# Block 1's second half of attention in 32-query tiles, transposed on VectorE

## The chip, the cores and the metric

The kernel runs on one core of a Trainium2 chip, in one launch. The metric is the device time of that core in microseconds (us). A program that sets out all instructions runs on five engines at once: TensorE (PE, with its weight loads as PEld), VectorE (DVE), ScalarE (ACT), GpSimd (POOL) and SyncE (SP), which here only issues DMAs. Each engine takes its own instructions strictly in order and waits where one of them needs a result of another engine.

## What is computed

Sparse attention, then two MLPs. Of eight heads the first four see a local window, the others a strided set:

```
scores = (1/sqrt(64)) * q @ k.T                     # q, k, v: (4, 8, 576, 64) float32
mask_local   = (rel >= 0) & (rel < 32)              # heads 0 to 3, rel = query - key
mask_strided = (rel >= 0) & (rel % 32 == 0)         # heads 4 to 7
attn = softmax(where(mask, scores, -1e9)) @ v
x = attn as (2304, 512)
x = (s * relu(x @ w_in)**2 + b) @ w_out             # 2048 wide
out = ((x @ w_a) * (x @ w_b)) @ w_out2              # 1536 wide
```

All products of the MLPs are made from pairs of reduced-precision halves: a high part (written by ScalarE) and the remainder (written by VectorE), in three matmul passes.

## The kernel before

**Blocks and calls.** The first MLP runs over five blocks of columns. Block 0 holds the first 128 positions of all four batches (512 columns), blocks 1 to 4 the other 448 positions of one batch each, give or take 64 (block 1 has 384). A block is 16 calls, one for each slice of 128 hidden rows: `h_mm` (12 matmuls into the single bank of `ps_h`, then `relu`, square and the split into `gt`, lines 773 to 789), `o_mm` of two calls earlier (12 matmuls into `acc`), and then `attend`, which runs whatever steps of the attention the plan has for that call.

**Weights.** In block 0 each call also turns two weight pieces from their 64-bit input form into halves: `raw` is scaled on ScalarE (line 130), shifted and merged by VectorE (lines 133, 136, 140), copied as the high half by ScalarE (line 111), and its remainder is taken by VectorE (line 112, `w<-raw,w`). The pieces of call f are used one and two calls later.

**Units.** The attention of a later block is made in six units while the block before it is computed: four local ones (two head pairs, two spans of positions each; `near` in `plan`) and two strided ones (two head pairs, all 448 positions; `far`). A unit is a generator of six or seven steps: loads, transposes of q and k, scores, softmax, softmax, transposes of the probabilities, output. The output goes through `split` into the next block's `x` tile: the high part by ScalarE, the remainder by VectorE.

**Two forms of a unit.** Block 1's units are `local` and `strided`, in 64-query tiles. Their q and k are transposed on TensorE (`pst`, line 97) and copied out of PSUM by ScalarE (lines 294, 337, 351). `local` lets a matmul write the mask into the scores' bank first, takes the maximum on VectorE (line 231) and makes four exponentials with running sums on ScalarE (line 237); `strided` adds the mask on VectorE (line 243) over 2 x 288 columns and goes on with 576-column steps (lines 244 to 254). The units of blocks 2 to 4 are `local_pairs` and `strided_pairs`, in 32-query tiles: q and k are loaded in 32 x 32 blocks and transposed by VectorE (`STREAM_TRANSPOSE`, lines 445, 501, 502), the mask is added on VectorE (line 419), and maximum, subtraction, sum, reciprocal and scaling (lines 426 to 433) stand on VectorE over 256 columns (local) or 288 (strided), with one exponential on ScalarE (line 428). The transposes of the probabilities and the output take fewer, larger or more, smaller matmuls.

**What sets the order.** `plan(n)` gives each unit a first call and a tuple of offsets; step k runs in call first + offset k:

```
near: 4 * i - 1, local(...) if n == 1 else local_pairs(...), at_n     # i = 0 to 3
far:  8 * i + 1, (strided if n == 1 else strided_pairs)(...), at_f    # i = 0, 1
```

TensorE's instructions keep this written order (`in_order`). The other engines' order is set by the scheduler of the framework, from its own estimate of when each instruction becomes ready; SP's too. Below, L1 to L4 stand for the local units `near[0]` to `near[3]` of block 1, S1 and S2 for `far[0]` and `far[1]`.

**Shared room.** PSUM has eight banks: four for `acc`, one for `h`, three for everything of the attention (`ps_a`, tag "a"), which each `pst`, `pss`, `ppt` and `po` takes in turn; a bank is free again when its last reader is done. The `r` tile of `h_mm` is single as well. The local units' `qk` has one buffer, the strided units' `sqk` one.

Of the kernel before, what the change touches and what calls it, by code (L numbers as in the profile page):

```python
# [25 lines left out]
def sparse_attention_two_mlps(  # L26
# [24 lines left out]
    TF = P  # L51
# [41 lines left out]
    def mm(*args, **kwargs):  # L93
        last_pe[:] = [nc.tensor.matmul(*args, **kwargs).ins]  # L94

    def mm_t(*args):
        last_pe[:] = [nc.tensor.transpose(*args).ins]  # L97
# [12 lines left out]
    def split(hi, lo, src):  # L110
        nc.scalar.activation(out=hi, in_=src, func=AF.Copy)  # L111
        return nc.vector.tensor_tensor(out=lo, in0=src, in1=hi.bitcast(F32), op=ALU.subtract)  # L112
# [45 lines left out]
    def x_tile(n):  # L158
        if n not in x_t:
            x_t[n] = xp[n % 2].tile([P, 2, KD, TR if n % 2 else TM], F32R, tag="x", name="x")  # L160
            if n and n % 2 == 0:
                nc.gpsimd.tensor_copy(out=x_t[n][:, :, :, 0:OVER], in_=x_t[n - 1][:, :, :, TR - OVER:])
        return x_t[n]

    def first_column(n):
        return OVER if n % 2 == 0 else 0

    QT = 64
# [89 lines left out]
    def window(src, bb, head, t0, nt):  # L258
        at = src[bb, head, t0:S, :]
        return bass.AP(at.tensor, at.offset, [[D, WK], [QT * D, nt], [1, D]])  # L260
# [10 lines left out]
    def local(bb, n, pair, t0, nt):  # L271

        nq, nk = nt * QT, nt * QT + STR
        mq, mk = (P, nk // 3) if nk % 3 == 0 else (nq // 2, nk // 2)
        cq, ck = nq // mq, nk // mk
        nu = -(-nt // 2)
        tl = lambda shape, name: lp.tile(shape, F32, tag=name, name=name)
        qk = tl([P, 5, 2, D], "qk")
        z = t0 + nq
        qn, kn = qk[:, 0:2], qk[:, 2:]  # L280
        for h in range(2):
            for dst, src, a, m in ((qn, q, t0, mq), (kn, k, t0 - STR, mk)):
                nc.sync.dma_start(
                    out=dst[:m, 0:(z - a) // m, h],
                    in_=src[bb, 2 * pair + h, a:z, :].rearrange("(c p) d -> p c d", p=m),
                )
        yield
        qkT = lp.tile([P, 9 * QT], F32, tag="lT", name="qkT")
        qT, kT = qkT[:, 0:nq], qkT[:, nq:nq + nk]
        for src, m, c, dst in ((qn, mq, cq, qT), (kn, mk, ck, kT)):  # L290
            ps = ps_a.tile([P, c, m], F32, tag="a", name="pst")
            for i in range(c):
                mm_t(ps[:, i], src[:m, i].rearrange("p h d -> p (h d)"), ident[:m, :m])
            nc.scalar.activation(out=dst.rearrange("p (c m) -> p c m", m=m), in_=ps, func=AF.Copy)
        yield
        vn = tl([WK, 4, 2, D], "vn")
        for h in range(2):
            nc.sync.dma_start(out=vn[:, 0:nt, h], in_=window(v, bb, 2 * pair + h, t0 - STR, nt))
        pss = [ps_a.tile([P, nu, WK], F32, tag="a", name="pss") for _ in range(2)]

        def put(alone):
            for j in range(2 * nu if alone else nt):
                i = min(j, nt - 1) * QT
                for h in range(2):
                    hr = slice(h * D, (h + 1) * D)
                    mm(
                        pss[h][j % 2 * QT:(j % 2 + 1) * QT, j // 2],
                        lhsT=qT[hr, i:i + QT], rhs=kT[hr, i:i + WK],
                        start=alone, stop=(alone or j >= nt - 2),
                    )  # L310

        pt = tl([P, 2, nu, WK], "lpt")
        yield from softmax(pt, pss, lmask, put, n == 1, pair == 0 and t0 == TF)
        yield
        ppt = ps_a.tile([WK, 2 * nu, P], F32, tag="a", name="ppt")
        for i in range(2 * nu):
            mm_t(ppt[:, i, :], pt[:, i // nu, i % nu], ident)
        pT = lp.tile([WK, 2, nu * P], F32, tag="lT", name="pT")
        nc.scalar.activation(out=pT.rearrange("p h t -> p (h t)"), in_=ppt.rearrange("p i t -> p (i t)"), func=AF.Copy)
        yield  # L320
        po = ps_a.tile([P, nq], F32, tag="a", name="po")
        for j in range(nt):
            for h in range(2):
                mm(
                    po[h * D:(h + 1) * D, j * QT:(j + 1) * QT],
                    lhsT=vn[:, j, h, :], rhs=pT[:, h, j * QT:(j + 1) * QT],
                    start=True, stop=True,
                )
        xt, c0 = x_tile(n), t0 - TF + first_column(n)
        split(xt[:, 0, pair, c0:c0 + nq], xt[:, 1, pair, c0:c0 + nq], po)  # L330
        yield
# [654 lines left out]
    steps = {}  # L986

    def plan(n):
        at_n = (-2, 0, 1, 1, 2, 3, 4) if n == 1 else (-3, 0, 1, 2, 3, 4)
        at_f = (-3, 0, 1, 2, 4, 5) if n == 1 else (-3, 0, 1, 2, 3, 5)  # L990
        near = [
            (
                4 * i - 1,
                local(0, n, i % 2, TF + i // 2 * 4 * QT, 4 - i // 2) if n == 1
                else local_pairs(n - 1, n, i % 2, TF + i // 2 * 8 * QS, 8 - i // 2 * 2),
                at_n,
            )
            for i in range(4)
        ]
        far = [(8 * i + 1, (strided if n == 1 else strided_pairs)(n - 1, n, i), at_f) for i in range(2)]  # L1000
        if n == 1:
            near[0] = (0, near[0][1], (-5, -3, 0, 1, 1, 2, 3))
            far[0] = (1, far[0][1], (-5, 1, 2, 3, 5, 7))
        if n == 2:
            near[0] = (-1, near[0][1], (-2, 0, 1, 2, 3, 4))
        for first_, gen, at in near + far:
            for t in at:
                steps.setdefault((n - 1) * NF1 + first_ + t, []).append(gen)
# [80 lines left out]
    for n in range(1, NB):  # L1089
        plan(n)  # L1090
# [91 lines left out]
    for pair in range(NP2):  # L1182
        acc = [ps_acc.tile([P, DM], F32, tag="acc", name="acc2") for _ in range(TB2 // P)]
        later_x, late = [], []
        for g in range(NG2):
            i = pair * NG2 + g
# [129 lines left out]
```

## Time and profile before

| | us |
|---|---|
| median of 3 runs (lowest, highest) | 900.36 (900.26, 900.46) |
| profiled execution: span from first to last instruction | 898.1 |
| median less span: lies around the span | 2.3 |
| TensorE busy in the span | 888.6 |
| VectorE busy | 620.5 |
| ScalarE busy | 401.4 |
| first `h` of block 0, first `h` of block 1 | 31.56, 134.13 |

No time of the profiled execution other than its span is listed; the table sets the span beside the median of the runs. Starts in a timeline are measured, the ends of matmuls are modelled, so the length of a piece of TensorE's work is read here from start to start. On VectorE, instructions that follow each other closely overlap by some 0.08 to 0.1 us in the rows: the next one starts that much before the modelled end of the one ahead.

### The profile page before, as it was taken

To read this page: it belongs to the slowest core of one execution; us is meant where nothing else is said; L and a number is where in the kernel's file an instruction comes from. 1 tells how busy PE (TensorE), PEld (TensorE's weight loads), DVE (VectorE), ACT (ScalarE), POOL (GpSimd) and SP (SyncE) were. 2 spreads that over 40 slices of the span, in tenths; PEclk is the share of its full clock that TensorE was granted. 3 is DMA by queue.
4 is the path that set the end of the run, shared out by engine and by line. 5 is a ranking of instruction groups with operands and counts; after the bars stand their busy time and mean duration, and the time that the engine had idled before them with its cause. 6 is when DMAs were issued, how large, how long until landed. Compare 5 with 4: busy or idle time off the path is not lost.

```text
span 898.1 us, 16348 instructions
## 1 busy us (share of the span) xinstructions
PE 888.6 (99%) x6166; PEld 793.8 (88%) x6166; DVE 620.5 (69%) x1263; ACT 401.4 (45%) x866; POOL 42.0 (5%) x120
## 2 busy tenths in 40 slices
PE   8999999999999999999999999999999999999997
PEld 6778889999888899998889999988999988999986
DVE  6898995676766777727665777765776765776741
ACT  6777774434333343353333445354334444333322
POOL 6000000000000010001100000000000000000000
PEclk9999999999999999999999999999999999999999
DMA  9965534656765666446666343423432221433010
GB/s 229 292 204 162 166 77 134 159 149 162 207 170 159 176 190 172 130 137 220 196 214 207 129 141 112 138 80 113 151 99 94 84 94 59 124 95 106 30 36 35
DMA packets 156606, 126.41 MB, mean 141 GB/s; under 512 B 102256, under 2 KB 131440, under 8 KB 156528
## 3 DMA queue, kind: packets, MB, share of 16 engines
q1 hardware_dynamic: 149840, 109.12, 43.3%
q0 software_dynamic: 4608, 15.73, 4.4%
q8 instruction: 48, 0.79, 0.4%
q10 hardware_dynamic: 2080, 0.52, 0.3%
q14 instruction: 30, 0.25, 0.1%
HBM read 100.17 MB, written 25.17 MB: 140 GB/s over the span
## 4 chain that ended last, share of the span: by engine, by line
PE 97%; ACT 2%; DVE 1%; issue 0%; POOL 0%; ACTq 0%; POOLq 0%
PE acc L94 38%; PE pp L94 29%; PE h L94 22%; PE po L94 2%; PE pss L94 1%; PE ppt L97 1%; PE fpo L94 1%; PE fps L97 0%; PE lull L94 0%; ACT raw L130 0%; ACT fpt L596 0%; PE fss L94 0%; PE pst L97 0%; PE fpp L97 0%; PE fpx L97 0%; ACT r L778 0%
## 5 line engine op out<-in xcount | busy, mean ns | idle before, releaser
L94 PE MATMUL pp<-x2w,wf 128*128 128x384 f32 x1512 | 265.8, 335 | 0.0
L94 PEld LDWEIGHTS pp<-x2w,wf 128*128 128x128 f32 x1512 | 263.0, 188 | 1.8 <-ACT u L596 0.4
L94 PE MATMUL h<-x,w 128*128 128x512 f32 (+1 forms) x960 | 217.0, 374 | 0.0
L94 PE MATMUL acc<-gt,w 128*128 128x512 f32 (+2 forms) x960 | 210.7, 368 | 1.0 <-ACT w L111 1.0
L94 PEld LDWEIGHTS acc<-gt,w 128*128 128x128 f32 x960 | 175.5, 188 | 24.1 <-ACT w L111 1.5
L94 PEld LDWEIGHTS h<-x,w 128*128 128x128 f32 x960 | 171.8, 188 | 24.2 <-DVE w L112 0.5
L94 PE MATMUL acc<-o2w,abt 128*128 128x512 f32 x648 | 150.5, 390 | 0.0
L94 PEld LDWEIGHTS acc<-o2w,abt 128*128 128x128 f32 x648 | 121.4, 188 | 24.6
L778 ACT ACTIVATE r<-h 128x512 f32<-128x512 f32 (+1 forms) x80 | 44.4, 554 | 153.2 <-PE h L94 144.4
L788 DVE TENSOR_TENSOR r<-r 128x384 f32<-128x384 f32 (+1 forms) x64 | 40.0, 625 | 91.2 <-ACT gt L785 91.1
L601 DVE TENSOR_TENSOR u<-pp,u 128x384 f32<-128x384 f32 x72 | 39.9, 555 | 64.8 <-PE pp L94 59.3
L596 ACT ACTIVATE u<-pp 128x384 f32<-128x384 f32 x36 | 17.7, 493 | 115.6 <-PE pp L94 115.6
L596 ACT ACTIVATE wf<-w2t 128x512 fp32r<-128x512 f32 x72 | 45.2, 628 | 21.2 <-PE pp L94 20.3
L601 DVE TENSOR_TENSOR wf<-w2t,wf 128x512 fp32r<-128x512 f32 x72 | 49.3, 685 | 0.3 <-ACT wf L596 0.3
L130 ACT ACTIVATE raw<-raw 128x512 f32<-128x512 f32 x66 | 42.7, 671 | 8.2 <-DMA raw<-in_moe_w_a_dram 6.6
L136 DVE SCALAR_TENSOR_TENSOR raw<-raw 128x512 uint32<-128x512 uint32 x66 | 44.4, 689 | 0.7
L789 DVE TENSOR_TENSOR gt<-r,gt 128x384 fp32r<-128x384 f32 (+1 forms) x64 | 40.0, 624 | 3.6
L601 DVE TENSOR_TENSOR wf<-w2r,wf 128x512 fp32r<-128x512 f32 x72 | 39.6, 549 | 0.0
L596 ACT ACTIVATE wf<-w2r 128x512 fp32r<-128x512 f32 x72 | 37.2, 517 | 4.5 <-PE pp L94 4.0
L601 DVE TENSOR_TENSOR abt<-dly,abt 128x384 fp32r<-128x384 f32 x36 | 19.8, 556 | 25.0 <-ACT abt L596 24.9
L596 ACT ACTIVATE abt<-c 128x384 fp32r<-128x384 f32 x36 | 18.9, 524 | 40.4 <-DVE c L601 40.4
L785 ACT ACTIVATE gt<-r 128x384 fp32r<-128x384 f32 (+1 forms) x64 | 36.5, 571 | 0.4
(149 smaller groups left out, 805.1 us busy)
## 6 DMA issues: line engine op xcount, KB each, us to landing
w2t<-w2s SPq DMA_DIRECT2D x36, 512.0 KB
w2r<-w2d SPq DMA_DIRECT2D x60, 256.0 KB
raw<-in_moe_w_out_dram SPq DMA_DIRECT2D x28, 512.0 KB
w2d<-w2s POOLq DMA_DIRECT2D x36, 256.0 KB, 4.3
raw<-in_moe_w_in_dram SPq DMA_DIRECT2D x16, 512.0 KB
raw<-in_moe_w_a_dram SPq DMA_DIRECT2D x12, 512.0 KB
raw<-in_moe_w_b_dram SPq DMA_DIRECT2D x12, 512.0 KB
w2s<-w2t POOLq DMA_DIRECT2D x12, 512.0 KB, 4.0
```

Of the source, the lines that this page charges most:

```text
L94: last_pe[:] = [nc.tensor.matmul(*args, **kwargs).ins]
L97: last_pe[:] = [nc.tensor.transpose(*args).ins]
L130: nc.scalar.activation(out=high.bitcast(F32), in_=high.bitcast(F32), func=AF.Copy, scale=HIGH_SCALE)
L136: nc.vector.scalar_tensor_tensor(out=low, in0=high, scalar=3, in1=low, op0=ALU.logical_shift_left, op1=ALU.bitwise_or)
L596: i = nc.scalar.activation(**kwargs).ins
L601: i = getattr(nc.vector, method)(**kwargs).ins
L778: relu = nc.scalar.activation(out=r, in_=ph, func=AF.Relu)
L785: nc.scalar.activation(out=hi, in_=r, func=AF.Square)
L788: nc.vector.tensor_tensor(out=r, in0=r, in1=r, op=ALU.mult)
L789: last = nc.vector.tensor_tensor(out=lo, in0=r, in1=hi.bitcast(F32), op=ALU.subtract)
```

## The change

Of block 1's units, L1, L2 and S1 stay as they were; L3, L4 and S2 become `local_pairs` and `strided_pairs`, with the offsets that the later blocks use. L2's last two steps (transposes of the probabilities, output) move from calls 6 and 7 to calls 7 and 8.

```diff
     def plan(n):
-        at_n = (-2, 0, 1, 1, 2, 3, 4) if n == 1 else (-3, 0, 1, 2, 3, 4)
-        at_f = (-3, 0, 1, 2, 4, 5) if n == 1 else (-3, 0, 1, 2, 3, 5)
+        old = lambda i, late: n == 1 and i < late
         near = [
             (
                 4 * i - 1,
-                local(0, n, i % 2, TF + i // 2 * 4 * QT, 4 - i // 2) if n == 1
+                local(0, n, i % 2, TF + i // 2 * 4 * QT, 4 - i // 2) if old(i, 2)
                 else local_pairs(n - 1, n, i % 2, TF + i // 2 * 8 * QS, 8 - i // 2 * 2),
-                at_n,
+                (-2, 0, 1, 1, 2, 4, 5) if i == 1 and old(i, 2) else (-2, 0, 1, 1, 2, 3, 4) if old(i, 2) else (-3, 0, 1, 2, 3, 4),
             )
             for i in range(4)
         ]
-        far = [(8 * i + 1, (strided if n == 1 else strided_pairs)(n - 1, n, i), at_f) for i in range(2)]
+        far = [
+            (
+                8 * i + 1, (strided if old(i, 1) else strided_pairs)(n - 1, n, i),
+                (-3, 0, 1, 2, 4, 5) if old(i, 1) else (-3, 0, 1, 2, 3, 5),
+            )
+            for i in range(2)
+        ]
```

L3's steps so stand in calls 4, 7, 8, 9, 10 and 11, L4's in 8, 11, 12, 13, 14 and 15, S2's in 6, 9, 10, 11, 12 and 14.

**TensorE, calls 7 to 9, before.** `h` and `acc` are a call's own matmuls; `pst` are L3's transposed q and k, `pss` scores, `po` outputs (`pT` L2's, `spT` S1's).

```order
L94 MATMUL h<-x,w 128x512 x12
L94 MATMUL acc<-gt,w 128x512 x12
L94 MATMUL po<-pT,vn 64x64 x8
L97 MATMUL pst<-ident,qk 128x96 x2
L97 MATMUL pst<-ident,qk 128x112 x2
L94 MATMUL h<-x,w 128x512 x12
L94 MATMUL acc<-gt,w 128x512 x12
L94 LDWEIGHTS ident_b
L94 MATMUL pss<-lmask_153,ident_b 128x192
```

Here L2's output and L3's transposes stand behind call 7; L3's mask, scores and S1's output behind call 8.

**TensorE, the same place with the change**, from L2's transposes behind call 7 on:

```order
L97 MATMUL ppt<-ident,lpt 96x128 x4
L94 MATMUL h<-x,w 128x512 x12
L94 MATMUL acc<-gt,w 128x512 x12
L94 MATMUL po<-pT,vn 64x64 x8
L94 MATMUL pss<-qkT 32x64 x16
L94 MATMUL po<-spT,sv 64x14x4 x16
L94 MATMUL h<-x,w 128x512 x12
L94 MATMUL acc<-gt,w 128x512 x12
```

L2's output, L3's scores and S1's output now stand together behind call 8, and nothing behind call 9. S1's output takes the bank of L3's first scores again, so it waits for the first L419 below.

**VectorE, from `gt` of call 8 to `gt` of call 9, before.** `raw` and `w` are weight work, `mx`, `sm` and `lpt` L3's softmax, `x<-po` the remainder of an output.

```order
L112 TENSOR_TENSOR gt<-r,gt 128x512
L133 TENSOR_SCALAR raw<-raw 128x512 x2
L232 TENSOR_SCALAR mx<-mx 128x2 x2
L112 TENSOR_TENSOR x<-po,x 128x448
L136 SCALAR_TENSOR_TENSOR raw<-raw 128x512 x2
L140 SCALAR_TENSOR_TENSOR raw<-raw 128x512
L252 TENSOR_SCALAR sm<-sm 128x4
L140 SCALAR_TENSOR_TENSOR raw<-raw 128x512
L253 RECIPROCAL sm<-sm 128x4
L254 TENSOR_TENSOR lpt<-lpt,sm 128x384
L112 TENSOR_TENSOR w<-raw,w 128x512 x2
L112 TENSOR_TENSOR gt<-r,gt 128x512
```

**VectorE, the same place with the change**, up to the weights' remainders (then L3's L430 to L433 and `gt` of call 9 follow); `qk` is L4's, `sqk` S2's:

```order
L112 TENSOR_TENSOR gt<-r,gt 128x512
L133 TENSOR_SCALAR raw<-raw 128x512 x2
L419 TENSOR_TENSOR lpt<-pss,lmask_155 128x2x64
L112 TENSOR_TENSOR x<-po,x 128x256
L419 TENSOR_TENSOR lpt<-pss,lmask_155 128x128
L445 STREAM_TRANSPOSE qkT<-qk 128x416
L136 SCALAR_TENSOR_TENSOR raw<-raw 128x512 x2
L426 TENSOR_REDUCE mx<-lpt 128x4
L501 STREAM_TRANSPOSE sqkT<-sqk 128x16x16x2
L140 SCALAR_TENSOR_TENSOR raw<-raw 128x512
L112 TENSOR_TENSOR x<-po,x 128x448
L140 SCALAR_TENSOR_TENSOR raw<-raw 128x512
```

Between the two `gt` there is now the whole of L3's softmax, L4's transpose and S2's two (L502 follows in the next rows), besides the remainders of L2's and S1's outputs.

**VectorE, from `gt` of call 14 on, with the change**; before, L4's scaling (L254 there) stood ahead of `gt` of call 13:

```order
L112 TENSOR_TENSOR gt<-r,gt 128x512
L133 TENSOR_SCALAR raw<-raw 128x512
L112 TENSOR_TENSOR w<-raw,w 128x512
L433 TENSOR_TENSOR lpt<-lpt,sm 128x256
L136 SCALAR_TENSOR_TENSOR raw<-raw 128x512
```

L4's last softmax step, L433, stands behind `gt` of call 14. On TensorE, L4's transposes (`ppt`) stand directly behind call 14's `acc` and ahead of S2's output.

## Rows read from the trace of the kernel before

**Rows 1.** The profile's page, parts 1 and 2: busy time; VectorE's busy tenths in 40 slices.

```profile
PE 888.6 (99%) x6166; PEld 793.8 (88%) x6166; DVE 620.5 (69%) x1263; ACT 401.4 (45%) x866; POOL 42.0 (5%) x120
...
DVE  6898995676766777727665777765776765776741
```

**Rows 2.** TensorE's waits over the whole span: line, releaser, us in total, times, longest.

```profile
PE lull L94 <- DVE ident_b L561: 2.9, 1, 2.9
PE acc L94 <- ACT w L111: 1.0, 1, 1.0
PE pss L94 <- ACT qkT L294: 0.7, 1, 0.7
```

**Rows 3.** Busy time by stretch: from:to, length, engines' busy us (instructions), clock, DMA share, GB/s.

```profile
120.81:134.13 13.32, 13.32 (x99) 10.75 (x96) 13.11 (x26) 10.14 (x21) 0.00 (x0) 1.00 0.49 100
sum 53.12, PE 53.12 PEld 42.88 DVE 48.81 ACT 38.91 POOL 0.00; mean PE 13.28 PEld 10.72 DVE 12.20 ACT 9.73 POOL 0.00
```

**Rows 4.** The same view, TensorE alone, stretches cut at the starts of its groups.

```profile
67.70:134.13 66.43, 66.43 (x451) 1.00 0.51 137
67.70:73.15 5.45, 5.45 (x25) 1.00 0.00 0
73.15:74.38 1.23, 1.23 (x13) 1.00 0.00 0
80.05:80.66 0.61, 0.61 (x17) 1.00 0.97 343
87.31:88.39 1.08, 1.08 (x35) 1.00 0.74 285
139.20:139.59 0.39, 0.39 (x34) 1.00 0.54 68
148.75:149.76 1.01, 1.01 (x67) 1.00 0.06 14
159.15:159.94 0.79, 0.79 (x37) 1.00 0.00 0
168.46:169.83 1.37, 1.37 (x68) 1.00 0.82 233
193.51:194.09 0.58, 0.58 (x25) 1.00 0.00 0
114.43:120.81 6.38, 6.38 (x34) 1.00 0.27 44
120.01:120.81 0.80, 0.80 (x9) 1.00 0.06 8
```

**Rows 5.** The same view, VectorE alone, from call 13's `gt` to call 14's.

```profile
122.31:127.19 4.88, 4.88 (x10) 1.00 0.68 111
```

**Rows 6.** Groups by shape, VectorE, 60 to 205 us: count | busy, mean ns | idle.

```profile
L445 DVE STREAM_TRANSPOSE qkT<-qk 128x416 f32<-128x416 f32 x2 | 1.2, 602 | 0.0
L501 DVE STREAM_TRANSPOSE sqkT<-sqk 128x512 f32<-128x512 f32 x2 | 1.4, 707 | 0.0
L502 DVE STREAM_TRANSPOSE sqkT<-sqk 128x576 f32<-128x576 f32 x2 | 2.5, 1258 | 0.0
L419 DVE TENSOR_TENSOR lpt<-pss,lmask 128x128 f32<-128x128 f32 x8 | 1.9, 283 | 1.0 <-PE pss L94 1.0
L433 DVE TENSOR_TENSOR sqk<-sqk,sm 128x288 f32<-128x288 f32 x2 | 0.9, 459 | 0.1
```

**Rows 7.** VectorE's timeline: start, us, line, operation, tile, count [idle before <-releaser].

```profile
88.08 0.61 DVE L231 TENSOR_REDUCE mx<-pss 128x2 f32<-128x192 f32 x2
88.61 0.68 DVE L112 TENSOR_TENSOR gt<-r,gt 128x512 fp32r<-128x512 f32 x1
...
114.56 0.75 DVE L445 STREAM_TRANSPOSE qkT<-qk 128x544 f32<-128x544 f32 x1 [0.78 <-DMA qk<-in_k_dram]
...
121.83 0.56 DVE L254 TENSOR_TENSOR lpt<-lpt,sm 128x384 f32<-128x384 f32 x1
```

**Rows 8.** Busy time of the span's first 3 us, all engines; granted clock behind POOL.

```profile
0.00:3.00 3.00, 0.08 (x1) 0.08 (x2) 1.21 (x1) 0.91 (x1) 2.36 (x16) 1.00 0.19 45
```

## The prediction

> **Names.** L1 to L4 are block 1's four local units, S1 and S2 its two strided ones. The change rewrites L3, L4 and S2 and moves L2's last two steps. Call f (0 to 15) is `h_mm(0, f)`, `o_mm` of call f−2 and `attend(f)`. Microseconds throughout; "estimate" marks what I worked out.
>
> **What bounds the kernel now.** First the busy shares: TensorE 99% of the span, and VectorE's fullest slices lie at its start, where the change lies [rows 1]. Then TensorE's waits: three in the whole span, 4.6 together [rows 2], and none in calls 6 to 15, where it is busy for 66.43 of 66.43 [rows 4]. So there a removed matmul is time won, as long as no engine behind TensorE becomes late. Next the stretch's busy times: from call 8 to the block's end VectorE works 48.81 of 53.12, and 13.11 of 13.32 in its last quarter; ScalarE has 14 to spare [rows 3]. VectorE is the engine to watch.
>
> **TensorE's part.** Calls 6 to 15 take 66.43; a call without attention takes 5.45, so attention costs 66.43 − 54.5 = 11.93 [rows 4]. With the change:
> - Calls 6 and 7: S1's eight transposes and L2's four, 1.23 together, now in two gaps.
> - Call 8: L2's output 0.61, L3's 32 score matmuls 0.39 (block 1's price), S1's output 1.08: 2.08.
> - Call 9: nothing. Call 10: two transposes of L3 and S2's 64 score matmuls, 1.01. Call 11: L3's output, 0.58. Call 12: L4's scores and S2's four transposes, 0.79. Call 13: nothing. Call 14: L4's two transposes and S2's output, 1.37. Call 15: L4's output, 0.58 [rows 4].
>
> Sum 7.64. Each gap also lengthens its neighbours: call 13 of before has 6.38 − 5.45 − 0.80 = 0.13 beyond its eight transposes [rows 4]. Eight gaps at 0.13 to 0.17 give 8.7 to 9.0, a saving of 2.9 to 3.2. I take 3.0: TensorE alone would start block 1 at 131.1 instead of 134.13. Gone are the input transposes of all three units and the mask matmuls of L3 and L4; the move of L2's steps by itself costs one more gap.
>
> **What VectorE must do.** A call's own work there (two weight pieces and `gt`'s remainder) is 4.88 [rows 5]. The units add: a transpose of 416 columns 0.60, S2's 0.71 and 1.26; masks, now added on VectorE, at 0.28 an instruction; further softmax steps at up to 0.46 [rows 6]. These are modelled lengths; back to back the next starts 0.08 to 0.1 earlier, S2's second transpose 0.16 earlier, and I use that spacing. Against this stand fewer columns: S2's softmax steps work on 288 columns, not 576. Net it is about 3 more, while TensorE's stretch gets 3 shorter; VectorE had 4.3 idle. That does not fit.
>
> I add up VectorE's row in its new order, from `gt` of call 8 to the instruction that frees L4's transposes (L433). Start: 88.61 in before [rows 7], less the two maxima ahead of it (88.61 − 88.08 = 0.53) and the 0.93 that TensorE is early by then: 87.15, an estimate. Behind it stand:
> - own work of calls 8 to 13: 6 × 4.88, less two weight remainders (0.6 each) that the order puts behind: 28.1; then `gt` of call 14, one shift, one remainder: 1.5;
> - L3's softmax 2.5, of which four steps run as a chain; L4's up to L433, 1.9; S2's 2.3;
> - transposes: S2 0.63 + 1.10, L4 0.52, block 1's next unit 0.66 (it was there before): 2.9;
> - remainders of L2's, S1's and L3's outputs: 1.2.
>
> Sum 40.4, nearly without holes: `gt` of every call is ready when its turn comes. L433 starts near 127.6 and ends near 128.05. TensorE, alone, would be at L4's transposes at 123.5 (131.1 less the 7.6 that follow: 1.37 + 5.45 + 0.2 + 0.58). It waits 4.5, in two places:
> - **Call 8.** S1's output matmuls are to reuse the PSUM bank of L3's first scores; they wait until VectorE has added the mask there (the first L419), which stands behind `gt` of call 8 and two shifts: near 88.7 instead of 86.7, a wait of 2.0. Behind it, the whole of calls 9 and on.
> - **Call 9** hides a third: ScalarE's `relu` of call 9 now stands behind L3's exponential and the weights of call 9, which wait for VectorE until about 94.5; call 10's `h` needs its single bank back, 95.2. TensorE, late by 2.0 already, comes there at 95.4.
> - **Call 14.** L4's transposes wait for L433: 125.5 to 128.05, 2.55. Before, L4 was scaled at 121.83 [rows 7], some 4 us ahead of the end of call 14's pair (120.81 + 5.45 [rows 4]).
>
> Block 1 starts at 128.05 + 7.6 = 135.7, against 134.13: **1.6 later**. From block 1 on the instructions stand as before, TensorE without waits, so the end moves by 1.6. The profiled span of 898.1 becomes 899.7; the median of 900.36 (2.3 around the span) becomes **902.0**.
>
> ScalarE loses the input copies and eight small exponentials; it only waits there, so I book no gain. On SP's queue (nothing of the change is on POOL's) each unit's loads become eight issues instead of four, S2's values sixteen instead of eight, and weights stand behind them. L4's loads can start when L3's transpose has read the buffer, S2's when S1's transposes are done, by 74.4 [rows 4]; VectorE takes both from about 89, so a lead of 10 us and more covers them. L3's lead is the shortest, under 1 us by my count. The weights behind the loads keep several us. I cost all this at nothing; without the cover it is rival 2.
>
> **What the Trainium skill says.** In "VectorE: DVE Perf Modes", Rules for kernel authors, a 32×32 transpose within banks is fastest on VectorE; by that rule the change is a plain gain and the time the first rival's. The trace agrees on the price (0.60 for 416 columns [rows 6]) but not on the gain, since the queue it joins is full [rows 3].
>
> **Rivals.**
> 1. *VectorE keeps up; the saving arrives.* 900.36 − 3.0 = **897.4**. It holds if L419 of L3 and L433 of L4 come before TensorE, that is if the row of 40.4 shrinks by 4.5. For: 4.3 idle, TensorE waits nowhere now. Against: most of that idle lies where VectorE waits for ScalarE's weights early in calls 8 to 10, and the new order fills only part. Chance 0.12. Between the two, a row 1.5 to 4 shorter than I have it leaves a wait of 0.5 to 3: 898 to 900.5. Chance 0.12.
> 2. *Loads come late.* VectorE's row takes a late transpose's wait in full; the one of before was 0.78 [rows 7]. Three of the kind are new: 0.8 to 2.3 on top, **902.8 to 904.3**. Against: the leads above. Chance 0.07.
> 3. *The clock falls in the new waits.* Matmuls at 1.2 GHz would take up to twice as long: for the pair behind L4's transposes up to 5.5 more, 903 to 907. Against: TensorE idled 2.9 at the start [rows 2] and the granted clock read 1.00, the 2.4 GHz level, in that stretch [rows 8]. Chance 0.03. The Trainium skill ("TensorE: Matmul & The Clock Gate", Why this matters for your kernels) warns of idle gaps over about 3 us; the waits that I forecast stay below that, and no run here has shown a fall.
>
> That the change does not do what it says is excluded: the order shows the new forms in place and nothing else moved after block 0.
>
> **How the numbers follow.** The forecast has 0.66. Its own range: the start at 87.15 may be off by 0.3, forty-odd rows by 0.02 each, hand-overs between engines add 0 to 0.3: 901.0 to 903.2. No change means within 0.2% (1.8), about what a measurement of this kernel can tell: 898.56 to 902.16. Of the forecast's 0.66 a little over half lies there (0.36), the rest above (0.30). The first rival is faster (0.12), the case between mostly the same (0.01 faster, 0.11 same), the second mostly slower, the third slower (0.09 slower, 0.01 same). Faster 0.13, same 0.48, slower 0.39. The range from 899.4 to 904.0 leaves out rival 1, half a tenth of the case between and the ends of rivals 2 and 3: less than 0.2.
>
> **What will show it.** Right: VectorE without holes from about 87 to 134; a wait of TensorE near 87 ended by L419 and one near 125.5 ended by L433, 4.5 together; block 1's first `h` near 135.7; calls 9 and 13 without attention on TensorE. If both waits are missing and block 1 starts near 131, rival 1 holds. A hole on VectorE ended by a DMA before L445 or L501 speaks for rival 2; a granted clock under 1.00 after 128 for rival 3. Wrong at the root would be a VectorE row well under 40.4 between those two instructions, or a difference that arises after block 0.

## The result, and the profile after the change

| | before | after |
|---|---|---|
| median of the runs (lowest, highest) | 900.26 (900.03, 900.46), 5 runs | 906.86 (905.06, 908.20), 5 runs |
| profiled execution: span | 898.1 | 905.8 (the run of 907.89) |
| first `h` of block 1 | 134.13 | 140.76 |

The ratio is 1.0073, 95% interval 1.0062 to 1.0084: slower by 6.6 us. The forecast was 902.0, the range 899.4 to 904.0. The direction was right, the size was not. The runs of after lie 3.1 apart, those of before 0.4. The mean granted clock of each run of after goes with its time: 0.996 at 905.06, 0.995 at 906.61, 0.994 at 906.86 and 907.89, 0.993 at 908.20.

The page's parts 1 and 2, after, against [rows 1]: TensorE is busy 2.7 longer, although the change takes some 3 us of work off it, and the granted clock has an 8.

```profile
PE 891.3 (98%) x6264; PEld 795.6 (88%) x6264; DVE 623.1 (69%) x1272; ACT 396.8 (44%) x847; POOL 41.9 (5%) x120
...
PEclk9999899999999999999999999999999999999999
```

TensorE's waits (line, releaser, us in total, times, longest): these two are new. Besides them and the three of [rows 2] there are four of 0.2 to 0.3.

```profile
PE ppt L97 <- DVE lpt L433: 2.3, 1, 2.3
PE po L94 <- DVE lpt L419: 2.0, 1, 2.0
```

They are the two waits of the forecast: ended by L419 and L433, 2.0 and 2.3 where 2.0 and 2.55 stood. TensorE's timeline shows their places, and what follows (start, us, line, operation, tile, shape, count, [wait <- releaser]):

```profile
88.68 2.01 PE L94 MATMUL po<-spT,sv 72*64 72x56 f32 x32 [1.98 <-DVE lpt L419]
90.62 5.45 PE L94 MATMUL h<-x,w 128*128 128x512 f32 x12
...
98.65 2.88 PE L94 MATMUL h<-x,w 128*128 128x512 f32 x12
...
131.30 0.41 PE L97 MATMUL ppt<-ident,lpt 128*128 128x128 f32 x2 [2.33 <-DVE lpt L433]
...
132.93 4.59 PE L94 MATMUL h<-x,w 128*128 128x512 f32 x12
...
140.18 0.66 PE L94 MATMUL po<-pT,vn 64*64 64x32 f32 x24
140.76 2.38 PE L94 MATMUL h<-x,w 128*128 128x384 f32 x12
```

S1's output starts at 88.68 (forecast 88.7). Behind it, `h` of call 9 takes 5.45 instead of 2.9, and from its start to that of `h` of call 10 pass 8.03; behind the second wait, `h` of call 15 takes 4.59. The granted clock by stretches of 2 us says why (from:to, length, TensorE's busy us (instructions), clock, DMA share, GB/s):

```profile
88.00:90.00 2.00, 1.32 (x25) 0.77 0.64 181
90.00:92.00 2.00, 2.00 (x16) 0.50 0.20 34
...
96.00:98.00 2.00, 2.00 (x11) 1.00 0.83 242
...
132.00:134.00 2.00, 2.00 (x62) 0.86 0.03 8
134.00:136.00 2.00, 2.00 (x6) 0.50 0.12 29
```

The clock falls to 0.50, the 1.2 GHz level, when the work behind the wait is under way, and is back at 1.00 from 96. Behind the second wait it falls again, between 133 and 134. VectorE's timeline (same columns) then has holes that the forecast did not have:

```profile
88.34 0.29 DVE L419 TENSOR_TENSOR lpt<-pss,lmask 128x128 f32<-128x128 f32 x1
...
99.06 0.69 DVE L112 TENSOR_TENSOR gt<-r,gt 128x512 fp32r<-128x512 f32 x1 [1.72 <-ACT gt L111]
...
104.40 1.29 DVE L112 TENSOR_TENSOR w<-raw,w 128x512 fp32r<-128x512 f32 x2 [1.56 <-ACT w L111]
...
130.73 0.43 DVE L433 TENSOR_TENSOR lpt<-lpt,sm 128x256 f32<-128x256 f32 x1
```

`gt` of call 9 waits 1.72 for ScalarE, whose `relu` waits for the slow `h`:

```profile
96.16 0.60 ACT L778 ACTIVATE r<-h 128x512 f32<-128x512 f32 x1 [1.63 <-PE h L94]
```

The weights of call 9 wait 1.56. So L433 starts at 130.73, not at 127.6.

**Where the time lies.** The profiled execution is 1.0 slower than the median, so its parts are not those of the 6.6 between the medians. In it block 1 starts 6.63 later than before. Up to there the parts are: the saving on TensorE (−2.8: the version without waits, below, starts block 1 at 131.00 and has 0.35 of L4's output left then), the two waits (1.98 and 2.33), the low clock behind the first (1.94 − 1.26 for S1's output and 98.65 − 90.62 = 8.03 against 95.81 − 90.23 = 5.58 from `h` of call 9 to `h` of call 10, the smaller numbers from the run with both waits filled: 3.1) and behind the second (140.18 − 132.93 = 7.25 against 5.68 from `h` of call 15 to L4's output: 1.6). Sum 6.2, measured 6.63. Call 6 already starts 0.15 later in this execution (67.85 against 67.70). The further 1.1 by which the spans differ (7.7) arises in blocks 1 and 2, with two waits of 0.2 and 0.3 among it; no run took it up.

### The profile page after: what moved, and what is told of

The parts are those of the page before. It is cut to its first block, busy times and chain, and to the rows that moved or that the text cites. A ratio compares the mean times of both kernels' runs of the same rounds, so it can differ in the third digit from the quotient of the medians.

```text
span 905.8 us, 16563 instructions
## 1 busy us (share of the span) xinstructions
PE 891.3 (98%) x6264; PEld 795.6 (88%) x6264; DVE 623.1 (69%) x1272; ACT 396.8 (44%) x847; POOL 41.9 (5%) x120
## 4 chain that ended last, share of the span: by engine, by line
PE 90%; DVE 4%; ACT 3%; DMA 2%; issue 0%; ACTq 0%; SPq 0%; DVEq 0%
PE acc L94 35%; PE pp L94 29%; PE h L94 21%; PE po L94 2%; PE pss L94 1%; PE ppt L97 1%; DMA raw<-in_moe_w_in_dram 1%; PE fpo L94 1%; ACT raw L130 1%; DVE w L112 1%; DMA fqk<-in_q_dram 1%; DMA raw<-in_moe_w_a_dram 1%; ACT fpt L596 1%; DVE raw L136 1%; DVE raw L140 0%; DVE raw L133 0%
## 5 line engine op out<-in xcount | busy, mean ns | idle before, releaser
L94 PE MATMUL h<-x,w 128*128 128x512 f32 (+1 forms) x960 | 221.1, 379 | 0.3 <-DVE x L112 0.3
L94 PEld LDWEIGHTS h<-x,w 128*128 128x128 f32 x960 | 174.7, 191 | 25.9 <-DVE x L112 0.7
L596 ACT ACTIVATE abt<-c 128x384 fp32r<-128x384 f32 x36 | 18.8, 523 | 40.4 <-DVE c L601 40.4
```

Source lines behind the costliest of these rows:

```text
L596: i = nc.scalar.activation(**kwargs).ins
```

## The experiments

The first theory: VectorE's full row makes two waits (as forecast), and behind each the clock falls; that lengthens VectorE's row too. Rival A: the clock falls for another reason (VectorE's load, the new order). Rival B: VectorE's row is longer than forecast by itself. Line numbers of a kernel shift by the lines that an edit inserts above them (L419 and L433 are L421 and L435 in the versions with filled waits, and in the one with less work on VectorE).

**1. Both waits filled.** `nought` holds zeros; the matmuls add them to `acc`.

```diff
+    def filler(number):
+        for _ in range(number):
+            mm(acc[0], lhsT=ident_b, rhs=nought[:, 0:1].to_broadcast([P, TM]), start=False, stop=False, ...)
+        yield
...
+        extra = [(0, filler(11), (14,))] * (n == 1), [(0, filler(9), (8,))] * (n == 1)
-        for first_, gen, at in near + far:
+        for first_, gen, at in extra[0] + near + extra[1] + far:
```

> The change with TensorE kept busy in its two new waits: 9 matmuls of 512 zero columns (added to acc, so they alter nothing) ahead of S1's output in call 8, 11 ahead of L4's transposes in call 14. Everything else is as in the change. Theory (two waits for VectorE of 2.0 and 2.5, and behind each the clock at its lower level, which also makes VectorE's row late): the granted clock stays 1.00, VectorE has no holes behind call 8, block 1 starts near 135.7 to 136.2, time 902.0 to 902.6. Rival A (the low clock has another cause than the waits, such as VectorE's load): the clock falls all the same, time 905 to 908. Rival B (VectorE's row is itself longer than the forecast, the clock is a side effect that costs little): clock 1.00, L433 of L4 still near 130, time 904.5 to 906.

Measured: 903.05 (902.23 to 903.64), ratio 1.0030, 1.0019 to 1.0042. TensorE's timeline and, below it, VectorE's:

```profile
86.91 2.13 PE L94 MATMUL acc<-nought,ident_b 128*128 128x512 bf16 x9
88.97 1.32 PE L94 MATMUL po<-spT,sv 72*64 72x56 f32 x32
90.23 3.02 PE L94 MATMUL h<-x,w 128*128 128x512 f32 x12
...
136.37 2.38 PE L94 MATMUL h<-x,w 128*128 128x384 f32 x12
```

```profile
87.36 0.68 DVE L112 TENSOR_TENSOR gt<-r,gt 128x512 fp32r<-128x512 f32 x1
...
127.87 0.41 DVE L435 TENSOR_TENSOR lpt<-lpt,sm 128x256 f32<-128x256 f32 x1
```

The clock stays at 1.00 through block 0 (0.999 over the span), VectorE's row from `gt` of call 8 to the scaling of L4 is 127.87 − 87.36 = 40.5 (forecast 40.4), and block 1 starts at 136.37, 2.24 later than before; 0.42 of this was there at call 6 (68.12 against 67.70). Rivals A and B fall: with TensorE held up just as long, but at work, the clock does not fall, and 1.8 is left of the 6.63, where the forecast had 1.6. The medians differ by 2.9, a little more than expected. This execution (902.23) is the fastest of six, which lie in two groups, 902.2 to 902.6 and 903.5 to 903.6, all at mean clocks of 0.999 to 1.000. So the slower group's 1.1 is not of the clock; there is no trace of it, and its cause is open.

**2. One wait filled.** The same edit with one of the two fillers.

> The change with only the first wait filled (9 matmuls of zero columns ahead of S1's output in call 8). Theory: no low clock in call 9, VectorE without holes, L433 of L4 near 128 as forecast; the wait of 2.5 in call 14 stays and the clock falls behind it, about 1.7; block 1 starts near 137.8, time 903.8 to 905, some 2 to 3 below the change. If the fall behind the first wait is hidden by VectorE anyway: as the change, 906 to 907. If the fall behind the second wait costs nothing: as with both filled, about 903.

Measured: 903.29 (903.10 to 905.06), ratio 1.0038, 1.0026 to 1.0051. The profiled execution was the slowest of its five (905.06):

```profile
128.65 0.66 PE L97 MATMUL ppt<-ident,lpt 128*128 128x128 f32 x2 [2.32 <-DVE lpt L435]
...
131.09 4.88 PE L94 MATMUL h<-x,w 128*128 128x512 f32 x12
```

> The change with only the second wait filled (11 matmuls of zero columns ahead of L4's transposes in call 14). Theory: wait of 2.0 and low clock in call 9 as in the change, L433 near 130.7; the filled wait leaves the clock at 1.00 in call 15, so 1.7 is won: block 1 starts near 139, time 904.5 to 905.5. If the clock falls there without a wait (rival A): as the change, 906 to 907.

Measured: 903.52 (903.24 to 904.50), ratio 1.0037, 1.0024 to 1.0049. Its profiled execution was the fastest (903.24):

```profile
88.50 1.66 PE L94 MATMUL po<-spT,sv 72*64 72x56 f32 x32 [1.99 <-DVE lpt L421]
90.09 4.21 PE L94 MATMUL h<-x,w 128*128 128x512 f32 x12
```

In both profiles the unfilled wait keeps its fall and the filled one loses it: that part holds. The medians were less than I expected (903.8 to 905 and 904.5 to 905.5). With the first filled, three runs of five lie at 903.1 to 903.3, hardly above those with both filled; the other two are 1.5 to 2.0 slower. The profile of one of these has the fall (`h` of call 15 at 4.88, 2.6 in all: from L4's transposes to block 1 pass 10.57, against 7.93 with both filled). The mean clock is 0.996 in these two and 0.998 in the three faster ones, against 0.999 to 1.000 with both filled, so a shorter fall is likely in the three too; they have no trace. With the second filled, `h` of call 9 takes 4.21 in the profile, not 5.45, and block 1 starts 1.0 later than with both filled. In the medians either wait left unfilled costs 0.2 to 0.5, both together 3.8: the prices don't add up, and no run shows why. What a fall costs differs from one execution to the next; the mean clocks of the result say that this is the likely reason why the runs of after spread by 3.1.

**3. The steps moved off the waits.** The first pair of lines moves S1's output, the others L4's transposes and S2's output; run alone, and together:

```diff
-            far[0] = (1, far[0][1], (-5, 1, 2, 3, 5, 7))
+            far[0] = (1, far[0][1], (-5, 1, 2, 3, 5, 8))
+            near[3], far[1] = (11, near[3][1], (-3, 0, 1, 2, 4)), (9, far[1][1], (-3, 0, 1, 2, 3, 6))
-        for first_, gen, at in near + far:
+        for first_, gen, at in near + far + [(11, near[3][1], (4,))] * (n == 1):
```

> The change with L4's transposes and S2's output in call 15 instead of 14 (order there: L4's transposes, S2's output, L4's output). The wait in call 8 stays. Theory: wait of 2.0 and low clock in call 9 as in the change (5.5 together); L433 near 130.7 is in time for call 15, so no second wait and no second fall; block 1 starts near 136.8, time 902.7 to 903.5. Rival A: the clock falls near 132 without a wait, time 904.5 or more. If the first wait's 5.5 had been hidden behind L433 anyway: below 901.

Measured: 901.92 (900.04 to 902.90), ratio 1.0016, 1.0007 to 1.0025; a little under what I expected.

```profile
88.46 1.94 PE L94 MATMUL po<-spT,sv 72*64 72x56 f32 x32 [1.98 <-DVE lpt L419]
90.33 3.95 PE L94 MATMUL h<-x,w 128*128 128x512 f32 x12
...
132.44 0.38 PE L97 MATMUL ppt<-ident,lpt 128*128 128x128 f32 x2
```

One wait, one fall (`h` of call 9 at 3.95), and L4's transposes without a wait in call 15. Three of the eleven executions (900.04, 900.66 and 901.15) have a mean clock of 0.999, like runs without a fall; the others have 0.996 to 0.998. So the fall behind this wait is likely, not certain.

> The change with S1's output in call 9 instead of 8, so that it no longer stands behind the first L419. Theory: no wait in call 8, no low clock in call 9; TensorE is back at the no-wait pace and meets L433 of L4 (which the scheduler now puts ahead of gt of call 14, near 126.3) in call 14 after a wait of 2.5 to 3; the clock falls behind that one, 1.7 more; block 1 starts near 135.6, time 901.5 to 903. If the first fall was not what made VectorE late (rival B), L433 comes near 129 and the time is 904 to 906. If the clock falls without a wait (rival A): as in the change, about 906.

Measured: 904.69 (904.10 to 906.11), ratio 1.0050, 1.0037 to 1.0063. A miss: the wait of call 8 is gone, and a longer one has come in call 10, where nothing was expected; the one of call 14 is down to 0.70.

```profile
102.52 0.44 PE L97 MATMUL ppt<-ident,lpt 128*128 128x128 f32 x2 [3.40 <-DVE lpt L433]
...
103.66 4.47 PE L94 MATMUL h<-x,w 128*128 128x512 f32 x12
```

> Both edits: S1's output in call 9, L4's transposes and S2's output in call 15. Theory: no wait of TensorE, clock 1.00 throughout; L433 near 126 to 128, needed only at about 129.5; block 1 starts near 131.1 to 131.6, time 897.4 to 898.0, the saving of 3.0 on TensorE in full and faster than the kernel before. Rival A (low clock not owing to waits): it falls near 90 or 132 all the same, 900 or more. Rival B (VectorE's row too long by itself): a wait of 1 to 2 in call 15, 899 to 901.

Measured: 902.78 (901.11 to 904.13), ratio 1.0032, 1.0020 to 1.0044. The same miss. VectorE's timeline, and TensorE's:

```profile
95.49 0.37 DVE L430 TENSOR_REDUCE sm<-lpt 128x4 f32<-128x256 f32 x1
...
99.93 0.66 DVE L112 TENSOR_TENSOR gt<-r,gt 128x512 fp32r<-128x512 f32 x1
...
101.78 0.41 DVE L433 TENSOR_TENSOR lpt<-lpt,sm 128x256 f32<-128x256 f32 x1
```

```profile
102.25 0.44 PE L97 MATMUL ppt<-ident,lpt 128*128 128x128 f32 x2 [3.38 <-DVE lpt L433]
...
103.31 3.04 PE L94 MATMUL h<-x,w 128*128 128x512 f32 x12
```

L430 of L3 runs at 95.49, but with S1's output moved the scheduler put the next steps of the chain between weight pieces, and L433 behind `gt` of call 10, at 101.78. L3's transposes wait for it from 98.87. In this execution (901.11, the fastest of its six) the clock stayed at 1.00 behind a wait of 3.38; in the version of one move it fell behind one of 3.40 (`h` at 4.47). The mean clock of the other five is 0.997 to 0.998, so it is likely to have fallen there.

**4. Less work on VectorE.** `light` is set for the pieces made in calls 8 to 13; shift and merge are left out there:

```diff
     def to_float32(r, out=None):
...
+        if light:
+            return high.bitcast(F32)
...
+                light[:] = [1] * (8 <= f <= 13)
```

> The change with less work on VectorE: the weight pieces made in calls 8 to 13 are taken from the scaled high words as they are, without shift and merge (lines 133, 136, 140 left out; some 3.0 less on VectorE in each of the six calls). Theory (the queue's length sets the second wait, the place of the first L419 behind gt of call 8 sets the first): a wait near 2 in call 8 stays, with the low clock behind it; L433 of L4 comes before 124, so no wait in call 14 and no fall behind it; block 1 starts near 136.6, time 902 to 903.5. If L433 is late because of the chain through ScalarE's exponential or a late load: still a wait of over 1.5 in call 14, 905 or more.

Measured: 902.34 (899.84 to 902.77), ratio 1.0016, 1.0007 to 1.0025.

```profile
89.28 1.55 PE L94 MATMUL po<-spT,sv 72*64 72x56 f32 x32 [2.36 <-DVE lpt L421]
90.76 4.37 PE L94 MATMUL h<-x,w 128*128 128x512 f32 x12
...
127.87 0.38 PE L97 MATMUL ppt<-ident,lpt 128*128 128x128 f32 x2
```

As expected: the second wait goes when VectorE's row gets shorter, the first stays (2.36), with its fall. The length of the row sets the one, the place of L419 in it the other.

**5. A version without waits.** Both moves of experiment 3, S2's transposes of the probabilities in call 13, and the weight pieces of call 10 ordered behind L3's L433 (`scaled` holds that instruction):

```diff
-                with after(behind + (last_w if f == 1 else []) or last_act + last_dve):
+                with after(behind + (last_w if f == 1 else scaled if f == 10 else []) or last_act + last_dve):
```

> A version meant to have no wait at all: S1's output in call 9, S2's transposes of the probabilities in call 13, L4's transposes and S2's output in call 15, and the weight pieces of call 10 ordered behind L3's L433, so that this stands ahead of gt of call 10 and L3's transposes find it done (near 98.1, needed at 98.9). Theory: no wait over 0.5, clock 1.00, block 1 starts near 131.0 to 131.4, time 897.3 to 898.2, the saving of 3.0 in full. If VectorE's row by itself is too long (rival B): a wait of 1 or more in call 13 or 15, 898.5 to 901. If the clock falls without a wait: 900 or more.

Measured: 897.97 (897.43 to 898.83), ratio 0.9973, 0.9962 to 0.9984: faster than before by 2.4.

```profile
98.84 0.38 PE L97 MATMUL ppt<-ident,lpt 128*128 128x128 f32 x2
...
131.00 1.51 PE L94 MATMUL h<-x,w 128*128 128x384 f32 x7
...
192.25 0.55 PE L94 MATMUL po<-pT,vn 64*64 64x32 f32 x20 [1.01 <-DVE sqk L419]
```

No wait in calls 6 to 15, the clock there at 1.00, block 1 at 131.00: about 2.8 of the 3.0 of TensorE's part are real, since 0.35 of L4's output stands behind the first `h`. In this execution, the slowest of seven, 1.8 of the 3.1 gained there are lost by the start of block 2 (212.78 against 214.14 before): those 0.35, and 1.0 is the wait in the last row, for a bank of the next strided unit's scores; 0.4 is open. VectorE is late there behind ScalarE, which waits 4.47 for a piece of the second MLP's weights (line 130, at 188.58).

**6. The wait by itself.** The kernel before, with a pause of TensorE at the end of call 9:

```diff
+    def pause(number):
+        for k in range(2):
+            mm(acc[0], lhsT=ident_b, rhs=nought[:, 0:1].to_broadcast([P, TM]), start=False, stop=False, ...)
+            for _ in range(number * (k == 0)):
+                nc.gpsimd.memset(nought, 0.0)
+        yield
...
-        for first_, gen, at in near + far:
+        for first_, gen, at in near + far + [(0, pause(14), (9,))] * (n == 1):
```

> The same with 6 memsets: a pause of about 0.8 to 1. The kernel before has waits of 0.7 and 1.0 near its start with the granted clock at 1.00, and the no-wait version lost 1.0 in block 1 with the clock at 1.00. Theory: no fall, before plus the pause, 901.0 to 901.5. If any wait brings the fall: 902.5 or more.

> The kernel before, without any part of the change, with a pause of TensorE at the end of call 9: a matmul of zero columns, 14 small memsets of its source on GpSimd (idle there), and a second such matmul that waits for them; about 1.5 to 2 us. Theory (a wait of TensorE of this size is by itself followed by the lower clock): the granted clock falls soon behind the pause, h of call 10 takes 1 to 2.6 longer; the time is that of before plus the pause plus 1.5 to 3.5, so 903.2 to 906. Rival (the fall in the changed kernel comes from VectorE's load or the changed order, not from the wait): clock 1.00, before plus the pause alone, 901.8 to 902.5.

> The same with 30 memsets: a pause of about 3 to 3.5. Theory: the clock falls behind it as behind the 2 us, the fall costing no more than there: before plus the pause plus 1.5 to 3.5, so 904.8 to 907.3; in some executions it may stay at 1.00, as behind the 3.4 us of the version with both steps later. Rival (no link with the wait): 903.3 to 903.9.

The memsets took longer than I thought: pauses of 1.83, 3.50 and 6.83. Medians 902.82 (902.70 to 903.46), 905.58 (904.42 to 905.79) and 909.55 (909.20 to 910.19); with these lengths the theory's sums for the longer two are 905.2 to 907.2 and 908.5 to 910.5, and both hold. The pause and the `h` behind it, in the three:

```profile
97.00 0.38 PE L94 MATMUL acc<-nought,ident_b 128*128 128x512 bf16 x1 [1.83 <-POOL nought L997]
97.03 3.10 PE L94 MATMUL h<-x,w 128*128 128x512 f32 x12
```

```profile
98.81 0.38 PE L94 MATMUL acc<-nought,ident_b 128*128 128x512 bf16 x1 [3.50 <-POOL nought L997]
98.84 4.69 PE L94 MATMUL h<-x,w 128*128 128x512 f32 x12
```

```profile
102.15 0.58 PE L94 MATMUL acc<-nought,ident_b 128*128 128x512 bf16 x1 [6.83 <-POOL nought L997]
```

and the clock in the longest, which fell during the pause:

```profile
98.00:100.00 2.00, 0.00 (x0) 0.96 1.07 376
100.00:102.00 2.00, 0.00 (x0) 0.50 0.64 158
```

With no part of the change in the kernel, the clock falls behind the two longer pauses: from the first `h` behind the pause to block 1 (134.13 before) 1.8 and 2.3 are lost beyond the pause and the 0.4 of the two matmuls (139.88 − 134.13 − 3.50 − 0.4; 143.71 − 134.13 − 6.83 − 0.4). It did not fall behind 1.83 (`h` 3.10; block 1 at 136.44, which is 134.13 + 1.83 + 0.4 and 0.1), and the mean clock of all five of its executions is 0.999 to 1.000. So a wait of 3.50 is enough for the fall without anything else of the change, and the fall costs about 2 here. That a wait of 2.0 or 2.3 is enough by itself is not shown: no pause of that length was made, and the nearest, 1.83, brought none. For the waits of the change the evidence is experiment 1. One of the four executions with 3.50 (904.42, mean clock 1.000) is likely to have had no fall either.

**7. The second part of the change alone**, in the kernel before:

```diff
-                at_n,
+                (-2, 0, 1, 1, 2, 4, 5) if n == 1 and i == 1 else at_n,
```

> The kernel before with the second part of the change alone: L2's transposes and output in calls 7 and 8 instead of 6 and 7. Theory: one more gap of TensorE at 0.13 to 0.17, no wait, clock 1.00: 900.3 to 900.7. If the move by itself makes a wait, say of L3's scores or S1's output for a bank that L2's output now holds longer: 1 to 2 more, and a fall of the clock behind it, 902 or more.

Measured: 904.62 (902.84 to 905.86), ratio 1.0048, 1.0034 to 1.0061. The theory missed by 4; the other case came.

```profile
87.28 0.48 PE L94 MATMUL pss<-lmask,ident_b 128*128 128x192 bf16 x2 [0.88 <-ACT qkT L294]
...
88.91 1.97 PE L94 MATMUL po<-spT,sv 72*64 72x56 f32 x32 [0.67 <-DVE x L112]
90.81 5.22 PE L94 MATMUL h<-x,w 128*128 128x512 f32 x12
```

L3's mask now waits 0.88 (the releaser, ScalarE's copy out of PSUM in L294, points to the bank), S1's output 0.67 for the remainder of L2's, and the clock falls with the two (`h` of call 9 at 5.22, 0.50 from 89 to 95). A third wait, of 0.48 for an exponential of ScalarE, comes at 125.72. In this execution (905.63) block 1 starts 5.3 later: the waits are 2.0 of it, the fall 3.0 (1.90 against 1.08 for S1's output, 7.81 against 5.60 from `h` of call 9 to S2's transposes). The fastest of the five, 902.84, has a mean clock of 1.000, so without a fall the move is worth about 2.6. In the changed kernel L3 has no such copies, so the price there is another; the run shows that a move "of one gap" can be worth 4.4.

## Why the prediction was wrong, point by point

- **TensorE's part**: right. Forecast 131.1 for block 1 without waits; the version that has none in calls 6 to 15 starts it at 131.00 with 0.35 of L4's output still to come, so 131.35.
- **What VectorE must do**: right in its sum. 40.5 in the run with the clock held, 40.4 forecast; 0.9 of the 40.5 is idle, so the work itself was taken a little too long and the holes too short. In after it is 43.7, of which 3.3 are the two holes of the slow calls.
- **Call 8 and call 14**: right in place, releaser and size (1.98 and 2.33 for 2.0 and 2.55, and 2.32 for the second with the first filled). In after both engines reach the second over 3 later than forecast, so that its size still fits there is partly luck. Rival 1 fell. "Call 9 hides a third": no wait there with the clock held; but where S1's output is moved, and no first wait hides anything, `h` of call 10 starts at 93.39 and 93.13 without a wait too (VectorE's order differs there), so nothing shows that there was one to hide.
- **Late loads** (rival 2): no hole of VectorE is ended by a DMA between 84 and 136; fell.
- **"From block 1 on … TensorE without waits"**: it held with both waits filled (2.24 later at block 1, 2.2 in the span), not in after, where 1.1 more is lost there.
- **"The clock falls in the new waits … Chance 0.03"**: this is the step that failed. The sum holds nothing for a lower clock; rival 3 is what came, behind both waits, at 3.1 and 1.6 in the profiled execution and 3.8 in the medians (906.86 against 903.05 with both waits filled). I argued from [rows 2] and [rows 8] that TensorE had idled 2.9 at the start with the clock at 1.00. The trace of before does not bear this out. TensorE's timeline there, and a stretch as in [rows 8] (TensorE alone):

```profile
2.92 2.74 PE L94 MATMUL lull<-ident_b 128*128 128x384 bf16 x8 [2.92 <-DVE ident_b L561]
...
29.85 1.46 PE L94 MATMUL lull<-ident_b 128*128 128x384 bf16 x8
```

```profile
3.00:5.00 2.00, 2.00 (x7) 1.00 1.31 256
```

The same eight matmuls take 2.74 behind that idle and 1.46 later, so TensorE came out of it at the pace of the lower level. The column prints 1.00 there all the same, because the trace's record of the clock begins only at 7.07. So the row was no evidence against rival 3; a clock column has to be checked against the time of equal matmuls. Whether that idle brought the clock down or it was low before the kernel began is not shown.

I also compared the two waits with the figure of the Trainium skill ("TensorE: Matmul & The Clock Gate", Why this matters for your kernels) one by one and found both shorter. The trace disagrees: the fall came behind 1.98 and 2.33. The size that rival 3 gave (903 to 907) was for one fall, behind the second wait; that it holds 906.86, with two falls, is luck: for the call behind the first wait I had no price at all, nor for the holes that it makes on VectorE.
- **The sum**: without the falls the forecast stands at 902.0 and the run with both waits filled at 903.05, its fastest three executions at 902.2 to 902.6. The 1.1 between the medians is open.
- **The move of L2's steps "costs one more gap"**: in the kernel before it costs 4.4, by three waits of under 1 that the sum did not have, and a fall of the clock with two of them. Whether it costs more than a gap inside the change was not run.

## What to carry to other kernels

Where TensorE never waits, a new wait can cost more than its length: here the lower clock behind waits of about 2 us cost 1.5 to 3.1 us more in the profiled executions, and likely nothing in some other executions. Keep a chance for it in the forecast, and look for who is slowed by the slow calls in turn. Here the saving on the busiest engine was worth nothing until the steps that stood behind the next engine's row had been moved to where they are not waited for; four moved steps and one forced order turned +6.6 into −2.4. After each such move read the order of the other engine again: the scheduler rearranged VectorE's chain, and the wait came back one unit earlier.

## What was not expected of the hardware

- The granted clock fell with waits of 1.98 to 2.36, 3.40 and 3.50, during one of 6.83, and with two short ones in a row (0.88 and 0.67, with small attention matmuls around them); it stayed at 1.00 behind 1.83, 1.01, 0.70, and in one execution behind 3.38. By the mean clocks some executions of a version whose profile has a fall had none: three of eleven with L4's transposes moved, two of ten (899.84 and 900.06) with less work on VectorE. The length of a single wait does not decide by itself; what else does, the runs don't show.
- On short waits, the Trainium skill ("TensorE: Matmul & The Clock Gate", A second HAM failure mode: psum-queue depth-cycling) tells of brief idles between groups of matmuls, frequent enough that the clock goes down and up repeatedly. The run with L2's move agrees in that short idles can bring the clock down (`h` of call 9 takes 5.22); it has two of them and one fall, not a repeated one.
- The clock reads 0.50 mostly behind a wait, not in it, so the price falls on the large matmuls of the next call. It differs from execution to execution: 3.1 and 1.6 in the profile of after, 2.6 for the second wait with the first filled.
- While TensorE ran matmuls of a zero column, broadcast to 512, in both places, the clock stayed at 1.00 there and in the calls behind.
